# Start-up of a causal convolution with a leaky-ReLU MLP: the second part of x through SyncE in float32 and a GpSimd cast, w_in's far columns and second half behind VectorE's first diagonal

## Chip, cores and metric

One core of a Trainium2 chip. The metric is the device time of one execution in microseconds; the time before is the median of three runs, 681.38 us (681.14 to 681.41).

## What is computed

The input x is float32 of shape (8, 4096, 192): 8 sequences, 4096 tokens, 192 channels in 8 heads of 24. `weight` is (8, 7).

```
w   = softmax(weight, over the 7 taps)            # per head, with 1e-9 added to the sum
y   = sum over k of w[head, k] * x[t - 6 + k]     # causal, zeros ahead of the sequence
h   = y.reshape(32768, 192) @ w_in                # w_in  192 x 2048
g   = max(0.01 * h, h)
out = g @ w_out                                   # w_out 2048 x 192, out float32
```

## The kernel before, in words

**Tiling.** Two sequences (e = 0, 1) are worked on at a time. The 192 channels stand as three chunks c of 64; chunk c of both sequences fills the 128 partitions of the tile xt[rp][:, c, :], with time along the free dimension. A block is 512 tokens of both sequences. To have work for TensorE early, the first two blocks are cut into four groups of 256 tokens, x's first four parts (q = 0 to 3); then whole blocks of 512 follow, 34 groups in all.

**Per group.** VectorE convolves seven taps (`conv_jobs`, L222 for the first tap and L228 for the others, which multiply by columns of wk, the normalized taps), TensorE makes h in PSUM from w_in and y (`mm1`, L507), ScalarE takes it out with Prelu (L515), and TensorE multiplies by w_out (L525 for the first blocks, L588 later), interleaved with the next `mm1`. The convolution of group i+1 is recorded during group i.

**How the parts of x come in.** Part 0 comes over SyncE in float32 (L142), is cast by ScalarE and VectorE (L155), transposed by TensorE and convolved by TensorE too, with diagonal matrices `diag` made from the taps by VectorE (`diag_wide`, L420; the matmuls are L259). Parts 1 and 2 are loaded by GpSimd with a cast during the DMA into `x_rows` (L145), transposed by TensorE (`transpose_first`, L167) and taken out of PSUM by VectorE (`evac_first`, L195). Part 3 and all blocks after it are loaded by GpSimd (L149, L96) and transposed by DMAs of SyncE (L199, L114).

**Weights.** w_in is kept in two halves n of 1024 columns. Rows 0 to 127 go into slot 0 over all partitions and rows 128 to 191 into slot 2 of the lower 64 (`load_w_in`, L316). VectorE, and once ScalarE, copy 64-partition pieces to the other half of the partitions (`spread_up`, L326; `spread_down`, L322), so that each row tile of TensorE finds every chunk. The first half's columns are again split in `near` (the first 512) and `far`.

**What sets the order.** Each engine works through its instructions in the order in which the kernel records them; there is no scheduler (`manual_schedule`), and waits come from data dependences, from `sync`, which adds one by hand, and from the reuse of eight semaphores for GpSimd's DMAs in turn, so that a DMA waits for the landing of the one eight before it. GpSimd's order in the start-up is: select for `sel`; w_in 0 rows 0 to 127 (all 1024 columns); `ident` by a memset and an affine select in `make_identity`; w_in 0 rows 128 to 191 near; x part 1 (two DMAs); w_in 0 rows 128 to 191 far; w_in 1 (two DMAs); x part 2 (two); w_out (two); wk (a sum and a product, L445 and L446); x part 3 (six); block 2 (six).

VectorE's order, after the small work on the taps, is: six diagonals (L420); L326 and L322 for the near columns of w_in 0; y of part 0, chunk 0 (L465); L326, L276, L326; the evacuation of part 1's transposes (L195, twice); L326 for rows 128 to 191 far; the first three taps of part 1's chunk 1 (L222, L228, L228); L322 and L326 twice for the second half of w_in; the remaining taps with one more L326 among them; then y of part 1 from TensorE's convolution of chunks 0 and 2 (L271, L276).

TensorE's order is: warm-up matmuls, the taps' broadcast, the transposes and the convolution of part 0, then `mm1` for group 0 with the transposes of part 1 inside its first pair of column blocks. Its fifth pair is the first that uses the second half of w_in.

Of the kernel before, what the change touches and what calls it, by code (L numbers as in the profile page):

```python
# [10 lines left out]
FP32 = mybir.dt.float32  # L11
BF16 = mybir.dt.bfloat16
# [3 lines left out]
def kernel(  # L16
# [8 lines left out]
    nc = tc.nc  # L25

    B, S, D = x.shape
# [13 lines left out]
    HS = SUB // 2  # L41
    NFC = F // 128
# [3 lines left out]
    RUN = 4  # L46
# [10 lines left out]
    const_pool = ctx.enter_context(tc.tile_pool(name="const", bufs=1))  # L57
    stage_pool = ctx.enter_context(tc.tile_pool(name="stage", bufs=2))
# [17 lines left out]
    x_nat, x_bf, xt = {}, {}, {}  # L76

    def sync(after, first, why):
        tc.add_manual_dep(
            after.ins, first.ins.name,  # L80
            mybir.DependencyInfo(
                mybir.DependencyClass.Sync, mybir.DependencyReason.DATA
            ),
            reason=why,
        )
# [36 lines left out]
    def new_xt(rp):  # L122
# [10 lines left out]
    x_rows = {  # L133
        q: const_pool.tile([128, 2, HS, D], BF16, name=f"x_rows{q}") for q in (1, 2)
    }

    def load_first(q):
        rows = x[0:2, q * HT : (q + 1) * HT, :].rearrange("e (s p) d -> p e s d", s=HS)
        if q == 0:
            x_nat[q] = stage_pool.tile([128, 2, HS, D], FP32, name="x_nat")  # L140
            for s in range(HS):
                nc.sync.dma_start(out=x_nat[q][:, :, s], in_=rows[:, :, s])  # L142
        elif q in x_rows:
            for e in range(2):
                nc.gpsimd.dma_start(out=x_rows[q][:, e], in_=rows[:, e])  # L145
        else:
            for c in range(NCH):
                for e in range(2):
                    nc.gpsimd.dma_start(  # L149
                        out=x_half[q][:, c, :, e, :],  # L150
                        in_=rows[:, e, :, c * CH : (c + 1) * CH],
                    )

    def cast_first(q, s, copy, e=slice(0, 2)):
        copy(  # L155
            out=x_half[q][:, :, s, e, :],
            in_=x_nat[q][:, e, s, :].rearrange("p e (c k) -> p c e k", c=NCH),
        )
# [76 lines left out]
    def y_of(grp, c):  # L235
        blk, t0, T = grp
        if blk not in yt:
            yt[blk] = yt_pool.tile([128, NCH, ST], BF16, name="yt")
        return yt[blk][:, c, t0 : t0 + T]
# [47 lines left out]
    w9 = const_pool.tile([H, K + 1], FP32, name="w9")  # L287
    nc.scalar.dma_start(out=w9[:, 0:K], in_=weight)  # L288
    load_first(0)

    ones = nc.const_aps.tensor(1.0, [128, ST], BF16)
# [7 lines left out]
    for sign, off in ((1, 0), (-1, GRP - 1)):  # L299
        nc.gpsimd.affine_select(  # L300
            out=sel[:, :, 0, :], in_=sel[:, :, 0, :], compare_op=mybir.AluOpType.is_ge,
            fill=0.0, base=off, channel_multiplier=-sign * GRP,
            pattern=[[sign * CH, NCH], [sign, CH]],
# [8 lines left out]
    near, far = slice(0, WF // 2), slice(WF // 2, WF)  # L312

    def load_w_in(n, rows, cols=slice(0, WF)):
        ps, slot = ((0, 128), 0) if rows == 0 else ((0, CH), 2)
        nc.gpsimd.dma_start(  # L316
            out=w_in[n][ps[0] : ps[1], slot, cols],
            in_=moe_w_in[rows : rows + ps[1], n * WF + cols.start : n * WF + cols.stop],
        )
# [8 lines left out]
    def w_in_of(f, e, c, m0, m1):  # L328
# [5 lines left out]
        ]  # L334

    load_w_in(0, 0)
    ident = const_pool.tile([128, 128], BF16)
    make_identity(nc, ident)
    load_w_in(0, 128, near)
    load_first(1)  # L340
    load_w_in(0, 128, far)
    for rows in (0, 128):
        load_w_in(1, rows)
    load_first(2)


    w_out = const_pool.tile([128, NFC, D], BF16)
    for h in range(2):
        cs = slice(h * NFC // (2 * RUN), (h + 1) * NFC // (2 * RUN))
        nc.gpsimd.dma_start(  # L350
            out=w_out.rearrange("p (c i) d -> p c i d", i=RUN)[:, cs],
            in_=moe_w_out.rearrange("(c p i) d -> p c i d", p=128, i=RUN)[:, cs],
        )


    wa = psum_h.tile([128, 2, ST], FP32, name="warm", tag="ph")
# [1 line left out]
    def warm(n, cols=HT, to=wa[:, 0]):  # L358
# [10 lines left out]
        out=nmax, in_=w9[:, 0:K], axis=mybir.AxisListType.X,  # L369
# [3 lines left out]
        out=w9[:, 0:K], in_=w9[:, 0:K], func=mybir.ActivationFunctionType.Exp,  # L373
# [18 lines left out]
    def select(out, parts):  # L392
# [10 lines left out]
    wps_hm = wps_hm[:, :, 0]  # L403
    new_xt(0)
    cast_first(0, 0, nc.scalar.copy)
    cast_first(0, 1, nc.scalar.copy, slice(0, 1))
    cast_first(0, 1, nc.vector.tensor_copy, slice(1, 2))
    taps = const_pool.tile([128, NCH, 2, K + 1, 2], BF16, name="taps")
    nc.vector.tensor_copy(
        out=taps, in_=wps_hm[..., None].to_broadcast([128, NCH, 2, K + 1, 2])  # L410
# [5 lines left out]
    def diag_wide(c, p):  # L416


        shape = [128, K, CH // 2, 2]
        nc.vector.tensor_mul(  # L420
            diag[c][:, p].rearrange("p k (m t) -> p k m t", t=2),
            ident2.rearrange("p (m t) -> p m t", t=2)[:, None].to_broadcast(shape),
            taps[:, c, p, 0:K, None, :].to_broadcast(shape),
        )
# [6 lines left out]
    evac_first(0, nc.scalar.copy, nc.scalar.copy)  # L431
    wml = const_pool.tile([128, NCH, K + 1], FP32, name="wml")
    rsum = const_pool.tile([128, NCH, 1], FP32)
    diag_wide(0, 0)
    diag_wide(0, 1)
    nc.vector.tensor_add(wml, wps_l, taps[:, :, 1, :, 0])
    diag_wide(1, 0)
    nc.vector.scalar_tensor_tensor(
        out=rsum, in0=wml[:, :, K:], scalar=1e-9, in1=taps[:, :, 0, K:, 0],
# [14 lines left out]
    def act_scale(out, in_, scale):  # L454
# [11 lines left out]
        out=y_of(groups[0], 0), in0=hi[:, :HT], scalar=rsum[:, 0, :], in1=low,  # L466
# [301 lines left out]
```

## Time and profile before

| what | value |
|---|---|
| runs: median (lowest to highest) | 681.38 us (681.14 to 681.41) |
| span of the profiled execution, first to last instruction | 679.2 us |
| median of the runs less that span | 2.2 us |
| granted TensorE clock, mean | 1.000 |
| first `mm1` matmul starts | 8.09 us |
| x part 1: issues start; landings | 3.62 and 4.34 us; 7.48 and 8.00 us |
| w_in 0 rows 0 to 127: issue starts; lands | 1.87 us; 6.33 us |
| w_in 1, its two DMAs: land | 12.19 and 12.77 us |
| HBM read, written | 28.31 MB, 25.17 MB |

The profile shows one execution. Times are counted from the span's start; a DMA's landing is the last update of its semaphore. PEld is the loading of weights into TensorE, which overlaps its matmuls (PE). A row of the order of time gives start and duration in microseconds, engine, line, operation, tiles written and read, and how many such instructions were merged; in brackets stand the idle time ahead of it and what ended it. For a DMA on GpSimd the duration is that of its issue (descriptors written), not of the transfer.

### The profile page before, as it was taken

How to read it: one execution, taken by the hardware profiler on the slowest of the kernel's cores; microseconds unless marked ns; L12 is line 12 of the kernel's file. 1: busy time of each engine (PE TensorE's matmuls, PEld its weight loads, DVE VectorE, ACT ScalarE, POOL GpSimd, SP SyncE). 2: the span in 40 equal slices, each digit the busy share in tenths (PEclk: the TensorE clock that was granted, in tenths of full speed). 3: DMA queues.
4: the chain of work that ended last, by engine and by line, in shares of the span. 5: the costliest groups of instructions: out<-in, count | busy, mean ns of one | idle time of the engine just before them, and what ended most of it. 6: DMA issues, size and time to landing. Idle time of an engine off the chain costs nothing.

```text
span 679.2 us, 27092 instructions
## 1 busy us (share of the span) xinstructions
PE 674.9 (99%) x12442; PEld 446.3 (66%) x12442; DVE 481.2 (71%) x816; ACT 517.6 (76%) x601; POOL 147.4 (22%) x208
## 2 busy tenths in 40 slices
PE   9999999999999999999999999999999999999998
PEld 6997666666666666666666666666666666666667
DVE  7989477866768766778667687667786676876612
ACT  7899877777787777777777777778777777777781
POOL 8455221122211222211222112222022220000000
PEclk9999999999999999999999999999999999999999
DMA  9999755655737656556556566567365573321123
GB/s 149 99 119 104 52 85 83 84 64 67 96 74 93 76 54 86 84 85 86 66 63 92 80 92 78 56 83 94 73 87 69 60 96 71 72 56 33 34 49 94
DMA packets 213970, 53.27 MB, mean 78 GB/s; under 512 B 209312, under 2 KB 213536, under 8 KB 213856
## 3 DMA queue, kind: packets, MB, share of 16 engines
q0 software_dynamic: 98832, 13.97, 30.3%
q1 hardware_dynamic: 115008, 37.57, 28.0%
q8 instruction: 97, 1.59, 0.9%
q14 instruction: 17, 0.14, 0.1%
q10 hardware_dynamic: 16, 0.00, 0.0%
HBM read 28.31 MB, written 25.17 MB: 79 GB/s over the span
## 4 chain that ended last, share of the span: by engine, by line
PE 98%; DVE 1%; ACT 0%; issue 0%; ACTq 0%
PE ph L507 49%; PE acc L588 44%; PE po L525 5%; PE acc L259 0%; DVE diag L420 0%; PE ptr L167 0%; ACT L366 0%; ACTq L288 0%; DVE w_in L322 0%; DVE yt L465 0%; DVE o_sb L638 0%; DVE x_half L155 0%; ACT w L372 0%; DVE w_in L326 0%; ACT junk L366 0%
## 5 line engine op out<-in xcount | busy, mean ns | idle before, releaser
L515 ACT ACTIVATE g<-ph 128x1024 bf16<-128x1024 f32 x512 | 496.6, 1021 | 139.8 <-PE ph L507 139.6
L228 DVE SCALAR_TENSOR_TENSOR yt<-xt,wk,yt 128x512 bf16<-128x512 bf16 (+1 forms) x582 | 380.1, 715 | 0.2
L507 PE MATMUL ph<-yt,w_in 64*64 64x512 bf16 (+2 forms) x6048 | 377.5, 369 | 0.3 <-DVE yt L465 0.3
L588 PE MATMUL acc<-g,w_out 64*64 64x512 bf16 x5568 | 339.9, 376 | 0.0
L507 PEld LDWEIGHTS <-w_in 64*64 64x64 bf16 (+1 forms) x6048 | 229.7, 131 | 103.4 <-issue 1.1
L588 PEld LDWEIGHTS <-w_out 64*64 64x64 bf16 x5568 | 178.2, 118 | 118.8
L96 POOL DMA_DIRECT2D x_bf<-in_x_dram x180 | 133.9, 774 | 407.6 <-DMA xt<-x_bf 405.6
L610 DVE STREAM_TRANSPOSE o_t<-acc 128x512 f32<-128x512 f32 x87 | 72.9, 875 | 182.2 <-PE acc L588 182.2
L525 PE MATMUL po<-w_out,g 64*128 64x192 bf16 (+1 forms) x640 | 36.8, 243 | 0.0
L525 PEld LDWEIGHTS <-g 64*128 64x128 bf16 (+1 forms) x640 | 32.6, 95 | 3.2 <-issue 0.4
L222 DVE TENSOR_SCALAR yt<-xt,wk 128x512 bf16<-128x512 bf16 (+1 forms) x97 | 28.8, 320 | 2.4 <-DMA xt<-x_bf 2.4
L598 ACT COPY junk<-junk 128x1 f32<-128x1 f32 x58 | 11.1, 191 | 4.1
L638 DVE COPY o_sb<-po 128x192 f32<-128x192 f32 x8 | 2.8, 356 | 6.8 <-PE po L525 3.9
L638 ACT COPY o_sb<-po 128x192 f32<-128x192 f32 x16 | 5.1, 323 | 0.3
L259 PE MATMUL acc<-xt,diag 64*64 64x256 bf16 x126 | 4.7, 272 | 0.1
L149 POOL DMA_DIRECT2D x_half<-in_x_dram x6 | 4.3, 732 | 0.9 <-DMA w_in<-in_moe_w_in_dram 0.9
L259 PEld LDWEIGHTS <-diag 64*64 64x64 bf16 x140 | 3.7, 106 | 1.0 <-issue 0.4
L360 PE MATMUL warm<-const-bfloat16-1.0 128*128 128x512 bf16 (+2 forms) x8 | 3.3, 577 | 0.8 <-PEq L752 0.8
L145 POOL DMA_DIRECT2D x_rows<-in_x_dram x4 | 2.9, 746 | 0.0
L316 POOL DMA_DIRECT2D w_in<-in_moe_w_in_dram x5 | 2.9, 593 | 0.0
L360 PEld LDWEIGHTS <-const-bfloat16-1.0 128*128 128x128 bf16 x10 | 1.2, 128 | 2.2 <-issue 2.2
L326 DVE COPY w_in<-w_in 64x512 bf16<-64x512 bf16 (+1 forms) x7 | 2.3, 337 | 0.2
(52 smaller groups left out, 25.9 us busy)
## 6 DMA issues: line engine op xcount, KB each, us to landing
out_dram<-o_t SPq DMA_DIRECT2D x112, 192.0 KB, 4.7
x_bf<-in_x_dram POOLq DMA_DIRECT2D x180, 64.0 KB, 3.1
out_dram<-o_sb SPq DMA_DIRECT2D x8, 192.0 KB, 2.8
xt<-x_bf SPq DMA_TRANSPOSE x90, 3.2
w_out<-in_moe_w_out_dram POOLq DMA_DIRECT2D x2, 384.0 KB, 8.3
out_dram<-o_t SPq DMA_DIRECT2D x8, 96.0 KB, 2.4
out_dram<-o_sb SPq DMA_DIRECT2D x8, 96.0 KB, 1.7
w_in<-in_moe_w_in_dram POOLq DMA_DIRECT2D x2, 256.0 KB, 5.5
```

The lines of the kernel that those rows point to most:

```text
L96: ins = nc.gpsimd.dma_start(out=t[:, c, :, e, :], in_=src[2 * rp + e, :, :, c * CH : (c + 1) * CH],)
L222: lambda s=src, d=dst, c=c: nc.vector.tensor_scalar_mul(d, s, wk[:, c, 0:1])
L228: lambda s=src, d=dst, c=c, k=k: nc.vector.scalar_tensor_tensor(out=d, in0=s, scalar=wk[:, c, k : k + 1], in1=d, op0=mybir.AluOpType.mult, ...
L259: lambda k=k, p=p, a=a, ps=ps, to=to, acc=accs[e]: nc.tensor.matmul(out=acc[to, :T], lhsT=diag[c][ps, p, k, :], rhs=xt[0][ps, c, a : a + T ...
L360: nc.tensor.matmul(out=to[:, 0:cols], lhsT=ones[:, 0:128], rhs=ones[:, 0:cols], start=True, stop=True,)
L507: nc.tensor.matmul(out=ph[m : m + M, e, i * T : (i + 1) * T], lhsT=w_in_of(f, e, c, m, m + M), rhs=y[ps, c, t0 : t0 + T], start=(c == chun ...
L515: act = nc.scalar.activation(out=g[blk][:, nf * u : nf * (u + 1), :, t0 : t0 + T], in_=ph.rearrange("p e (i t) -> p i e t", i=nf), func=my ...
L525: return nc.tensor.matmul(out=po[m], lhsT=g[b][ps, fc, e, s * 128 : (s + 1) * 128], rhs=w_out[ps, fc, :], start=start, stop=stop,)
L588: ins = nc.tensor.matmul(out=acc2[gi, r][e * CH : (e + 1) * CH, 0:T], lhsT=w_out_of(ps, fc, r), rhs=g[b][ps, fc, e, t0 : t0 + T], start=fi ...
L598: seal = nc.scalar.copy(out=junk, in_=junk)
L610: nc.vector.transpose(out=osb[gi, 0][:, 0 : T // GB, :, r], in_=acc2.pop((gi, r))[:, 0:T].rearrange("p (j k) -> p j k", k=GB),)
L638: ins = copy(out=o_sb[:, n % 2, :], in_=po.pop(n))
```

## The change

- `load_first(1)` no longer goes through GpSimd with a cast during the DMA. SyncE issues two float32 DMAs, one per sequence, into a second `x_nat` buffer; the first waits for GpSimd's affine select that makes `ident`. `make_identity` is written out for that (a memset and the same select).
- GpSimd asks for w_in 0 rows 128 to 191 near as before. The far columns wait, by `sync`, for VectorE's first `diag_wide`; the second half of w_in follows.
- Then GpSimd casts the two float32 tiles into `x_rows[1]` with two copies of 128x384, and only then come x part 2, w_out, and what stood behind them.
- TensorE's transposes of part 1 wait for the two copies instead of the two DMAs. The order on TensorE, VectorE and ScalarE is the same.

```diff
+        elif q in (1,):
+            x_nat[q] = stage_pool.tile([128, 2, HS, D], FP32, name="x_nat")
+            for e in range(2):
+                ins = nc.sync.dma_start(out=x_nat[q][:, e], in_=rows[:, e])
+                if e == 0:
+                    sync(ins, after, "behind a nearer part")
...
     load_w_in(0, 0)
     ident = const_pool.tile([128, 128], BF16)
-    make_identity(nc, ident)
+    after = nc.gpsimd.memset(ident, 0.0)
+    after = nc.gpsimd.affine_select(
+        out=ident, in_=ident, compare_op=mybir.AluOpType.not_equal, fill=1.0,
+        base=0, pattern=[[-1, 128]], channel_multiplier=1,
+    )
+    load_first(1, after)
     load_w_in(0, 128, near)
-    load_first(1)
-    load_w_in(0, 128, far)
-    for rows in (0, 128):
-        load_w_in(1, rows)
-    load_first(2)
-    w_out = ...
...
-    diag_wide(0, 0)
+    gate = diag_wide(0, 0)
+    sync(load_w_in(0, 128, far), gate, "behind x's second part")
+    for rows in (0, 128):
+        load_w_in(1, rows)
+    for e in range(2):
+        nc.gpsimd.tensor_copy(out=x_rows[1][:, e], in_=x_nat[1][:, e])
+    load_first(2)
+    w_out = ...
     diag_wide(0, 1)
```

More of the change, by code (lines that the diff above doesn't have):

```diff
@@ L135, with load_first @@
     }
-    def load_first(q):
+    def load_first(q, after=None):
         rows = x[0:2, q * HT : (q + 1) * HT, :].rearrange("e (s p) d -> p e s d", s=HS)
@@ L154, in cast_first @@
     def cast_first(q, s, copy, e=slice(0, 2)):
-        copy(
+        return copy(
             out=x_half[q][:, :, s, e, :],
@@ L315, in load_w_in @@
         ps, slot = ((0, 128), 0) if rows == 0 else ((0, CH), 2)
-        nc.gpsimd.dma_start(
+        return nc.gpsimd.dma_start(
             out=w_in[n][ps[0] : ps[1], slot, cols],
@@ L337 @@
     ident = const_pool.tile([128, 128], BF16)
-    make_identity(nc, ident)
-    load_w_in(0, 128, near)
-    load_first(1)
-    load_w_in(0, 128, far)
-    for rows in (0, 128):
-        load_w_in(1, rows)
-    load_first(2)
[L347 to L353, printed above, removed]
+    after = nc.gpsimd.memset(ident, 0.0)
[4 more added lines that the diff above has]
+    load_first(1, after)
+    load_w_in(0, 128, near)
     wa = psum_h.tile([128, 2, ST], FP32, name="warm", tag="ph")
@@ L419, in diag_wide @@
         shape = [128, K, CH // 2, 2]
-        nc.vector.tensor_mul(
+        return nc.vector.tensor_mul(
             diag[c][:, p].rearrange("p k (m t) -> p k m t", t=2),
@@ L433 @@
     rsum = const_pool.tile([128, NCH, 1], FP32)
-    diag_wide(0, 0)
+    gate = diag_wide(0, 0)
[5 more added lines that the diff above has]
+    load_first(2)
+    w_out = const_pool.tile([128, NFC, D], BF16)
+    for h in range(2):
+        cs = slice(h * NFC // (2 * RUN), (h + 1) * NFC // (2 * RUN))
+        nc.gpsimd.dma_start(
+            out=w_out.rearrange("p (c i) d -> p c i d", i=RUN)[:, cs],
+            in_=moe_w_out.rearrange("(c p i) d -> p c i d", p=128, i=RUN)[:, cs],
+        )
     diag_wide(0, 1)
```

## The prediction

> **What bounds the kernel now.** I read the page first, then the windows by stage, then the order of time of GpSimd and VectorE in the first 16 us, and last who waits there.
>
> Page, part 1 (busy time, share of the span) and part 4 (the chain that ended last, by engine):
>
> ```profile
> PE 674.9 (99%) x12442; PEld 446.3 (66%) x12442; DVE 481.2 (71%) x816; ACT 517.6 (76%) x601; POOL 147.4 (22%) x208
> ...
> PE 98%; DVE 1%; ACT 0%; issue 0%; ACTq 0%
> ```
>
> TensorE is the bound: 674.9 of 679.2 us, at a granted clock of 1.00 throughout. From the first matmul on w_in (8.09 us) to the last stage it is never idle for long, so a microsecond can be won or lost only where it waits, before 8.09 and in the few waits shortly after. A stall there moves everything behind it, since nothing later is idle enough to give it back. The change touches only work of the first 16 us.
>
> Windows by stage (width, busy us of PE, PEld, DVE, ACT, POOL; clock; DMA share; GB/s):
>
> ```profile
> 0.00:8.09 8.09, 6.83 (x106) 4.36 (x107) 5.12 (x25) 4.92 (x12) 7.27 (x19) 1.00 0.79 133
> 8.09:16.50 8.41, 8.41 (x166) 6.43 (x167) 7.36 (x19) 7.40 (x10) 6.74 (x12) 1.00 1.19 165
> ```
>
> In both windows GpSimd is nearly full (7.27 of 8.09, 6.74 of 8.41): it is a queue of instructions in order, and whatever the change inserts pushes back all that stands behind. GpSimd in order of time (start, duration, what):
>
> ```profile
> 3.62 1.44 POOL L145 DMA_DIRECT2D x_rows<-in_x_dram  x2
> 5.03 1.67 POOL L316 DMA_DIRECT2D w_in<-in_moe_w_in_dram  x3
> 6.64 1.48 POOL L145 DMA_DIRECT2D x_rows<-in_x_dram  x2
> 8.05 1.48 POOL L350 DMA_DIRECT2D w_out<-in_moe_w_out_dram  x2
> 9.46 0.32 POOL L445 TENSOR_TENSOR wk<-taps,wml 128x21 f32<-128x21 bf16 x1
> 9.87 0.22 POOL L446 TENSOR_TENSOR wk<-wk,rsum 128x21 f32<-128x21 f32 x1
> 10.09 1.48 POOL L149 DMA_DIRECT2D x_half<-in_x_dram  x2
> 12.47 2.87 POOL L149 DMA_DIRECT2D x_half<-in_x_dram  x4 [0.91 <-DMA w_in<-in_moe_w_in_dram]
> ```
>
> The line to keep in mind is wk, done at 10.09. VectorE's convolution of the second part of x reads it:
>
> ```profile
> 9.88 0.36 DVE L326 COPY w_in<-w_in 64x512 bf16<-64x512 bf16 x1
> 10.26 0.29 DVE L222 TENSOR_SCALAR yt<-xt,wk 128x256 bf16<-128x256 bf16 x1
> 10.59 1.00 DVE L228 SCALAR_TENSOR_TENSOR yt<-xt,wk,yt 128x256 bf16<-128x256 bf16 x2
> 12.21 0.42 DVE L322 COPY w_in<-w_in 64x1024 bf16<-64x1024 bf16 x1 [0.61 <-DMA w_in<-in_moe_w_in_dram]
> 12.64 0.77 DVE L326 COPY w_in<-w_in 64x512 bf16<-64x512 bf16 x2
> ```
>
> wk has 0.17 us to spare before 10.26. Behind its three reads VectorE sits idle 0.61 us until w_in's second half lands, then spreads it over the partitions, and TensorE waits for exactly that:
>
> ```profile
> 13.46 1.02 PEld L507 LDWEIGHTS <-w_in 64*128 64x128 bf16 x19 [0.21 <-DVE w_in L326]
> ```
>
> Of these 0.21 us 0.11 is the ordinary step (12 such matmuls take 0.65 us, two at a time), so TensorE loses 0.1: it could have gone on at 13.36.
>
> **The change, part by part.**
>
> *x's second part by SyncE.* Removed from GpSimd: the two issues at 3.62 (to 5.03, 1.41 us). SyncE has nothing between 1.77 and 18.1 us, so nothing queues behind its wait for the select at 2.85+0.29 = 3.14; it issues at about 3.2 and 3.65 (0.45 each, as for x's first part). What arrives sooner is not what was late: by the landing records the two x_rows loads land at 7.48 and 8.00 (3.62 + 3.9, 4.34 + 3.7), TensorE's transposes start at 8.65. Gain on the path: nothing.
> Landing in float32: x's first part landed 2.6 us after each issue with the DMA engines almost empty, which gives 5.8 and 6.25; the most is the present 8.0, since the same bytes and w_in's first half are read from HBM either way. I take 7.2 for the second, between the two, because w_in's 512 KB are in flight until 6.33. The Trainium skill (DMA: Bandwidth & Descriptors, "Issuing engines are not separate DMA queues") speaks against a gain: DMAs of all issuers share the same engines and another issuer saves only the time to issue; by it x would land near 8.0, at the late end.
> w_in's first part lands at 6.33 and VectorE takes it at 6.67: 0.3 us of room for what x now takes from it. Beyond that each 0.1 us is 0.1 us at 8.09.
>
> *The gate.* The far columns wait for the first diagonal (4.52 + 0.39 = 4.91, start about 4.95, against 5.03 now): 0.08 us earlier, because the 1.41 us removed and the wait for 4.91 fill the same time. Behind the waiting instruction stand all later GpSimd work: w_in, casts, x's third part, w_out, wk. The three w_in issues take 6.64 - 5.03 = 1.61 and end at 6.56.
>
> *The casts, new on GpSimd.* The trace has no copy on GpSimd. Nearest rows: memsets of 128x128 and 128x192 at 228 and 258 ns give 0.35 us for 384 columns (lower bound); selects at 287 and 355 ns, which read and write, give 355 + 192 x 1.06 = 0.56; two selects of 192 give 0.71 (upper). I take 0.56, as a copy reads and writes too, with 0.07 between instructions: 1.25 for both, 0.8 to 1.5. They start at 6.6 if x has landed, or the second at 7.2 to 8.0 by the landing. They end at 7.8, or 7.8 to 8.6 by the landing; with some mutual blocking with VectorE's copies I take 8.0. TensorE's transposes need them at 8.65: 0.6 in hand.
>
> *What is queued behind the casts.* From the first issue of x's third part to wk's first instruction 9.46 - 6.64 = 2.82, wk itself 10.09 - 9.46 = 0.62. So wk is done at 8.0 + 2.82 + 0.62 = 11.44, L222 starts at 11.47 in place of 10.26: **1.21 us late.** From L222 to TensorE's resumption is 13.46 - 10.26 = 3.20, of which 0.61 is the wait for w_in; w_in is now there long before, so 2.59 remain: TensorE resumes at 14.06 in place of 13.46, **0.6 us late**. The wait for a DMA has turned into a wait for wk. The two do not add: 0.61 of the 1.21 is swallowed.
>
> *Mutual blocking.* Copy L322 of 64x512 at 6.97 took 550 ns, L326 of the same shape at 6.67 only 287; GpSimd was issuing x's third part (6.64 to 8.12). L326 of 64x1024 at 12.85 took 559, L322 of that shape 422. So GpSimd can hold up such a copy by 0.14 to 0.26 us. The casts now meet L326 and L322 at 6.67 and 6.97. At best the copies go unhindered (0.26 less), at worst each waits for a whole cast: 2 x 0.56 - 0.26 = 0.86 more. The first matmul then moves from 8.09 by -0.1 to +0.86 (no earlier than that, as the second chunk's scale on ScalarE ends only at 8.18). I take +0.2. It is covered: with TensorE waiting to 14.06, up to 0.7 us of lateness at 8.09 vanish in the same stall. Without that cover it would count in full. The Trainium skill (SBUF — State Buffer, "Who interferes with whom") says that a VectorE copy in a two-port mode and a GpSimd operation lock each other out for the whole instruction; the rows above show 0.26 at most, and by the rule the estimate would be the upper end.
>
> *x's third part, w_out, x_half.* Their issues come 1.3 us later. The third part is used at 15.98 and landed at 13.28 and 13.81. x_half's issues now wait 0.91 us for w_in and the next block's loads 0.68 and 1.08 us for w_out's landing; those waits swallow the delay, and w_out still lands behind the same bytes. I cost them at nothing; if w_out slipped, the first use is at 17.1, 1.4 after its first landing at 15.73.
>
> **Sum.** Removed issues and earlier landing 0; gate -0.08 (already in 8.0); wk +0.6; blocking covered. The page gives the span, 679.2; the runs' median is 681.38, 2.2 us more for what lies around it, which I take as fixed. 679.2 + 0.6 + 2.2 = **682.0 us**, +0.09%.
>
> **Rivals.**
>
> 1. *Hidden.* Casts at 0.35 us with x there by 6.6 end at 7.4; wk at 10.84, TensorE resumes at 13.46. For it: x landing 2.6 us after issue. Against: 0.56 from the select. Time 681.3.
> 2. *The start decides.* The casts block L326 and L322 in full, or w_in's first part lands past 6.67; the first matmul moves to 8.8 or 8.95 and less than that is left of the wk stall. For it: 550 against 287 ns. Time 681.38 + 0.8 = 682.2.
> 3. *Slower by over 0.2%: x starves.* x and w_in share the DMA engines, the second x lands past 8.2 and a cast takes 0.7 with blocking, so the casts end past 8.8. Then wk is past 12.2, TensorE resumes past 14.86, 1.4 late; from there each 0.1 us of landing costs 0.1. For it: DMA digits of 9 in the first two slices of the page. Against: the same bytes land by 8.00 today. Time 683.0.
> 4. *The change does nothing for x:* transposes were not waiting for it (8.00 against 8.65); this is part of the forecast, whose sign comes only from what the casts push back.
>
> **How the numbers follow.** wk late by a stall of 0.2 to 1.2 us: 0.62. Rival 1: 0.14. Rival 2: 0.09. Rival 3: 0.13. Something faster by over 0.2% (1.36 us, about what a measurement of this kernel can tell from no change): 0.02, since only 0.1 + 0.1 us of waits are there to win. Slower by over that: rival 3 with little else, 0.14. Within: 0.84. Range: from the unhindered end (681.38 - 0.2) to rival 3 (683.0): 681.1 to 683.0.
>
> **What would show it.** Right: two copies on GpSimd of about 0.5 us from 6.6 to 8.0; wk at about 11.4; L222 of VectorE waiting for POOL wk some 1 us; L322 of the second half with no wait for the DMA; TensorE's wait for DVE w_in of 0.8 in place of 0.21. Wrong: wk before 10.9, a first matmul after 8.9, transposes that wait for POOL, or a difference after 16.5 us.

## The result, and the profile after

The changed kernel takes 682.52 us (median of 14 runs, 682.14 to 682.89); the kernel before, run beside it, 681.01 (14 runs, 680.63 to 681.44). The ratio is 1.0021, with a 95% interval of 1.0014 to 1.0029: **1.5 us slower**. The profiled execution spans 680.9 us, 1.77 more than before. The lines of the changed kernel's program are about six to ten higher: `mm1` is L517, the first tap L228, the other taps L234, spread_up and spread_down L332 and L328, wk L455 and L456, y of part 0 L465 and L475.

The page of the kernel after, parts 1 and 4:

```profile
PE 675.5 (99%) x12442; PEld 447.4 (66%) x12442; DVE 481.7 (71%) x816; ACT 517.7 (76%) x601; POOL 146.8 (22%) x208
...
PE 93%; DVE 5%; POOL 1%; DMA 1%; issue 0%; SPq 0%; POOLq 0%
```

Busy times are those of before, 675.5 against 674.9, so the time went into waits. Part 4 says whose: the chain that ended last was 98% TensorE and 1% VectorE; now it has VectorE 5%, GpSimd 1% and a DMA 1%. Which, the windows by stage tell first (columns as in the prediction):

```profile
0.00:8.09 8.09, 7.05 (x110) 4.47 (x111) 5.10 (x25) 4.93 (x12) 4.94 (x16) 1.00 0.73 156
8.09:16.50 8.41, 7.42 (x143) 5.45 (x141) 5.95 (x16) 6.28 (x9) 8.33 (x14) 1.00 1.10 159
```

GpSimd has gone from 7.27 to 4.94 us in the first window and from 6.74 to 8.33, which is full, in the second; there TensorE has gone from 8.41 to 7.42. The chain of waits of the kernel after shows the path through that hole (start, length, what):

```profile
3.58 4.44 DMA x_nat<-in_x_dram
...
8.07 0.28 POOL x_rows L436
8.35 0.17 issue
8.52 1.43 POOL x_rows L151 x2
9.95 1.42 POOL w_out L441 x2
11.37 0.27 POOL wk L455
11.63 0.07 issue
11.70 0.23 POOL wk L456
...
11.96 0.30 DVE yt L228
```

x's second DMA lands at 8.02, the cast follows, then four DMA issues that nothing on this path needs, then wk, and only then VectorE's first tap. The two casts of this kernel in order of time, each started by a landing:

```profile
7.30 0.50 POOL L436 CAST x_rows<-x_nat 128x384 bf16<-128x384 f32 x1 [0.52 <-DMA x_nat<-in_x_dram]
8.07 0.51 POOL L436 CAST x_rows<-x_nat 128x384 bf16<-128x384 f32 x1 [0.26 <-DMA x_nat<-in_x_dram]
```

The other end of the chain, VectorE and then TensorE's weight loads in order of time:

```profile
9.84 0.29 DVE L332 COPY w_in<-w_in 64x512 bf16<-64x512 bf16 x1
11.96 0.29 DVE L228 TENSOR_SCALAR yt<-xt,wk 128x256 bf16<-128x256 bf16 x1 [1.82 <-POOL wk L456]
12.28 1.01 DVE L234 SCALAR_TENSOR_TENSOR yt<-xt,wk,yt 128x256 bf16<-128x256 bf16 x2
13.32 0.42 DVE L328 COPY w_in<-w_in 64x1024 bf16<-64x1024 bf16 x1
13.76 0.78 DVE L332 COPY w_in<-w_in 64x512 bf16<-64x512 bf16 x2
```

```profile
12.97 0.11 PEld L517 LDWEIGHTS <-w_in 64*128 64x128 bf16 x1 [0.20 <-issue]
14.26 0.15 PEld L517 LDWEIGHTS <-w_in 64*128 64x128 bf16 x4 [1.18 <-DVE w_in L332]
14.59 0.47 PEld L517 LDWEIGHTS <-w_in 64*128 64x128 bf16 x10 [0.18 <-DVE w_in L332]
```

L328 at 13.32 has no bracket: w_in's second half landed long before (10.21 and 10.86, where it was 12.19 and 12.77). The wait of 0.61 us for a DMA became one of 1.82 us for wk. TensorE stands 1.18 us ahead of 14.26, and what it did from 13.46 on it now does from 14.59 on.

Matching TensorE's matmuls one by one with those of before gives the whole sum, for these two executions:

| point in TensorE's program | after less before, us | what made it |
|---|---|---|
| first `mm1` | -0.28 (7.82 for 8.09) | L328 took 0.29 instead of 0.55 |
| from 9.1 to 13 us | -0.03 | the second chunk waits for ScalarE's L465 as before |
| resumption at 14.6 | +1.13 | the wait above |
| behind 47 us | +1.41 | VectorE's taps are late there too, in this execution |
| end of the span | +1.77 | SyncE's last waits |

The step at 47 us is in the chain of waits:

```profile
44.95 2.66 DVE yt L234 x4
47.61 0.04 issue
47.65 1.27 PE ph L517 x10
```

In before VectorE convolved without a gap from 17.9 to 46.16 and was done 0.1 us ahead of TensorE. Here it is 1.44 late and TensorE only 1.13, so TensorE waits 0.28. Of VectorE's lateness 1.13 came with the start. Another 0.10 came at 19 us, where one first tap took 456 ns for 286 and the next 322 for 515, and 0.23 at 34.58, where one took 577 ns for 335. GpSimd was issuing a load of the next block beside them (18.70 to 19.45, 34.25 to 35.04); that this is the cause was not tried, and a first tap of before took 335 ns beside such an issue (33.37 to 33.70). The step is not a steady effect of the change: in the traces of two other changed kernels that lost as much at 13 us (1.14 and 1.02, below "two output DMAs fewer" and "SyncE asks for x at once") it is 0.02 and 0.01, in a third ("the casts read x part 0") 0.27, and in one of a variant of the kernel before ("wk first in the kernel before") 0.18.

The last step lies behind TensorE's last matmul: from its start to the end of the span 3.57 us instead of 3.21. SyncE then goes through the semaphores of its DMAs in a fixed turn. From the two traces, the start of each of those waits (* is released by the last landing, the others had nothing to wait for or were released earlier):

```
before  677.00 .06 .12 .18 .25 .31 .37 .43  678.25*                       drain 678.32
after   678.41 .57 679.66*  .72 .79 .85 .91 .97 680.03                    drain 680.09
```

Each wait costs 0.06 us, even if its semaphore is long set. In before the last landing is at the last place; two more DMAs on SyncE (x part 1) move it on by two, to a place with six waits behind it, 679.66 to 680.03 or 0.37 us. The twelve profiled executions of this case agree: in the five kernels with two SyncE DMAs more than before the stretch behind the last matmul is 3.56 to 3.57 us, in the other seven 3.19 to 3.21.

### The profile page after: what moved, and what is told of

Its sections match the earlier page's. It is cut to its first block, busy times and chain, and to the rows that moved or that the text cites. A ratio compares the mean times of both kernels' runs of the same rounds, so it can differ in the third digit from the quotient of the medians.

```text
span 680.9 us, 27094 instructions
## 1 busy us (share of the span) xinstructions
PE 675.5 (99%) x12442; PEld 447.4 (66%) x12442; DVE 481.7 (71%) x816; ACT 517.7 (76%) x601; POOL 146.8 (22%) x208
## 4 chain that ended last, share of the span: by engine, by line
PE 93%; DVE 5%; POOL 1%; DMA 1%; issue 0%; SPq 0%; POOLq 0%
PE ph L517 46%; PE acc L598 44%; DVE yt L234 4%; PE po L535 3%; DMA x_nat<-in_x_dram 1%; DVE yt L228 0%; POOL x_rows L151 0%; POOL w_out L441 0%; DVE w_in L332 0%; DVE yt L282 0%; POOL sel L306 0%; POOL w_in L322 0%; DVE xt L201 0%; DVE w_in L328 0%; DVE yt L277 0%
## 5 line engine op out<-in xcount | busy, mean ns | idle before, releaser
L234 DVE SCALAR_TENSOR_TENSOR yt<-xt,wk,yt 128x512 bf16<-128x512 bf16 (+1 forms) x582 | 381.6, 730 | 0.2
L517 PE MATMUL ph<-yt,w_in 64*64 64x512 bf16 (+2 forms) x6048 | 378.3, 369 | 1.2 <-DVE w_in L332 1.0
L517 PEld LDWEIGHTS <-w_in 64*64 64x64 bf16 (+1 forms) x6048 | 230.3, 131 | 104.4 <-issue 1.5
L228 DVE TENSOR_SCALAR yt<-xt,wk 128x512 bf16<-128x512 bf16 (+1 forms) x97 | 29.7, 335 | 3.9 <-POOL wk L456 1.8
L322 POOL DMA_DIRECT2D w_in<-in_moe_w_in_dram x5 | 2.8, 567 | 1.6 <-DVE diag L417 1.6
L332 DVE COPY w_in<-w_in 64x512 bf16<-64x512 bf16 (+1 forms) x7 | 2.2, 328 | 0.2
```

The costliest lines, as they stand in the source:

```text
L228: lambda s=src, d=dst, c=c: nc.vector.tensor_scalar_mul(d, s, wk[:, c, 0:1])
L234: lambda s=src, d=dst, c=c, k=k: nc.vector.scalar_tensor_tensor(out=d, in0=s, scalar=wk[:, c, k : k + 1], in1=d, op0=mybir.AluOpType.mult, ...
L517: nc.tensor.matmul(out=ph[m : m + M, e, i * T : (i + 1) * T], lhsT=w_in_of(f, e, c, m, m + M), rhs=y[ps, c, t0 : t0 + T], start=(c == chun ...
```

## The experiments

Theory 1: GpSimd's queue. wk is late because casts, landing and issues stand ahead of it. Rival A: contention, x in float32 and w_in sharing the DMA engines, or the casts holding up VectorE. Rival B, found in the trace after: the end of the kernel, nothing to do with the start. All were run beside the kernel before; medians are of 11 or 12 runs.

**wk ahead of the casts.** The casts, x part 2 and w_out (not shown) go behind wk, the work is the same:

```diff
-    for e in range(2):
-        nc.gpsimd.tensor_copy(out=x_rows[1][:, e], in_=x_nat[1][:, e])
-    load_first(2)
...
     nc.gpsimd.tensor_add(wk, taps[:, :, 0, 0:K, 0], wml[:, :, 0:K])
     nc.gpsimd.tensor_mul(wk, wk, rsum.to_broadcast([128, NCH, K]))
+    for e in range(2):
+        nc.gpsimd.tensor_copy(out=x_rows[1][:, e], in_=x_nat[1][:, e])
+    load_first(2)
...
     load_first(3)
```

> The changed kernel with wk's sum and product ahead of the casts on GpSimd; casts, x's third part and w_out behind them. Theory 1 (queue): TensorE's stall of 1.2 us at 13 us is wk, pushed back by what the change puts ahead of it. Then wk runs at 6.8 to 7.4 us, while GpSimd waits for x anyway, VectorE's first tap (L222 of before) starts at about 10.2 instead of 11.96, TensorE's wait for VectorE's spread of w_in's second half goes from 1.2 us to 0.1 or nothing, VectorE has no late convolution at 47 us, and the time falls by 1.1 to 1.4 us to 681.1 to 681.4. The 0.36 us at the end of the profiled span stay. Theory 2 (contention): the float32 loads and the casts hold up w_in and VectorE's copies; moving wk takes less than 0.3 us off 682.5.

681.5 us against 681.0, ratio 1.0008 (0.9999 to 1.0016): 1.0 of the 1.5 us is gone. GpSimd and VectorE of this kernel in order of time:

```profile
6.80 0.27 POOL L445 TENSOR_TENSOR wk<-taps,wml 128x21 f32<-128x21 bf16 x1
7.14 0.22 POOL L446 TENSOR_TENSOR wk<-wk,rsum 128x21 f32<-128x21 f32 x1
7.84 1.10 POOL L448 CAST x_rows<-x_nat 128x384 bf16<-128x384 f32 x2 [0.48 <-DMA x_nat<-in_x_dram]
```

```profile
10.37 0.29 DVE L332 COPY w_in<-w_in 64x512 bf16<-64x512 bf16 x1
10.69 0.45 DVE L228 TENSOR_SCALAR yt<-xt,wk 128x256 bf16<-128x256 bf16 x1
```

wk fits into the time in which GpSimd waits for x, with 0.48 us of that wait left, and the first tap starts behind VectorE's own copy, with no wait. x landed no sooner (7.79 and 8.29). Of the 0.5 us that remain 0.36 is the end of the span, so what the late x costs by itself is too small to be seen here.

**Two output DMAs fewer.**

```diff
-            parts = 2 if gi == len(groups) // 2 else 1
+            parts = 2 if gi == len(groups) // 2 and e else 1
```

> The changed kernel with two output DMAs of SyncE fewer in the middle group, so that the number of SyncE's DMAs is that of before and the last one falls on the semaphore that it had there. If the 0.36 us at the end come from the order in which SyncE goes through its eight DMA semaphores (six more waits of 0.06 us behind the last landing), the time falls by 0.36 us to about 682.15 and the stretch behind the last landing is as long as before; TensorE's matmuls keep their 1.1 to 1.4 us. If the end is long because of anything else (a later landing, the outputs' DMAs), it stays at 682.5.

682.23 against 681.0, ratio 1.0019 (1.001 to 1.0027); 0.29 less than the changed kernel, and the trace has 3.20 us behind the last matmul instead of 3.57. The difference of the medians is less than half the spread of either kernel (0.75 and 0.69 us), so the trace carries this one.

**The same tail put on the kernel before,** by two more output DMAs:

```diff
-            parts = 2 if gi == len(groups) // 2 else 1
+            parts = (4 if e else 1) if gi == len(groups) // 2 else 1
```

> The kernel before with two more output DMAs of SyncE in the middle group (the same bytes cut finer), so that the last DMA falls two semaphores further on, as in the changed kernel. If the order of the last waits is what costs, +0.36 us (681.4), all of it behind the last landing, and TensorE's matmuls unmoved. Otherwise 681.0.

681.39 against 681.09, ratio 1.0003 (0.9995 to 1.0012); 3.56 us behind the last matmul. The median moved by 0.30, the tail in the trace by 0.35; the interval of the ratio alone would not exclude that nothing moved.

**Both repairs on the changed kernel.**

> Both edits. Theory 1: the two add, 682.5 - 1.1 to 1.4 - 0.36 = 680.75 to 681.05, at or a little under the time of before (681.0), since w_in's second half lands at 10.2 and 10.9 in place of 12.2 and 12.8 and TensorE's wait of 0.1 us for its spread can go. Theory 2: 682.1.

680.98 against 681.0, ratio 1.0004 (0.9993 to 1.0016; one of 12 runs, at 685.47, stands apart). TensorE's matmuls lie 0.26 us behind those of before at 12 us and 0.05 behind them from 16 us to the end, the span is 679.2, and part 4 is back to TensorE alone:

```profile
PE 99%; ACT 0%; DVE 0%; issue 0%
```

With wk's place and the last semaphore mended, the rest of the change costs and gains nothing that these runs can tell.

**wk first in the kernel before,** its sum and product moved ahead of x part 2 and w_out in the same way.

> The kernel before with wk's sum and product ahead of x's third part and w_out on GpSimd. Theory 1: wk at 7.3 us instead of 10.09 has no reader before 10.26, when VectorE comes free, and w_in's second half lands at 12.2 as before; no change within 0.15 us (681.0). It shows whether wk bound anything in the kernel before. If wk's place counts only where it is late, this is nothing while the same edit is worth over a microsecond in the changed kernel.

681.16 against 681.09, ratio 1.0001 (0.9992 to 1.0009). wk ended at 7.42 instead of 10.09 and nothing came of it: in before wk was not what VectorE waited for.

**The gate alone,** in the kernel before (x part 1 still by GpSimd):

```diff
-    load_w_in(0, 128, far)
-    for rows in (0, 128):
-        load_w_in(1, rows)
-    load_first(2)
...
-    diag_wide(0, 0)
+    gate = diag_wide(0, 0)
+    sync(load_w_in(0, 128, far), gate, "behind the first diagonal")
+    for rows in (0, 128):
+        load_w_in(1, rows)
+    load_first(2)
```

> The kernel before with the gate alone: w_in's far columns and second half behind VectorE's first diagonal, x's second part by GpSimd with the cast in the DMA as before. The gate as such costs GpSimd 0.15 to 0.25 us (it starts the far columns at about 5.2 instead of 5.03); wk is done at 10.3, VectorE's first tap at 10.3 instead of 10.26, and its wait for w_in at 12.2 swallows it: 681.0, no change within 0.15. If the gate itself were what cost the microsecond, 682.

681.1 against 681.09, ratio 1.0 (0.9991 to 1.0009). The diagonal ended at 4.975, the far issue began at 5.268, and wk ended at 10.38.

**SyncE asks for x at once,** without waiting for GpSimd's select:

```diff
-                if e == 0:
-                    sync(ins, after, "behind a nearer part")
```

> The changed kernel without the wait of SyncE for the select: x's second part is asked for at 1.8 and 2.2 us, right behind the first. Theory 1: it lands some 1 us or more before 7.25 and 8.02, the casts run from 6.8 to 7.9, wk is done at 11.25 in place of 11.92, and TensorE's stall is 0.6 us shorter: about 681.9. What it takes from w_in's first part shows as a later landing than 6.37; beyond 6.65 VectorE's first copy and the first matmul move, which the stall at 13 us covers. Theory 2: w_in's first part lands so late (past 7.5) that the first matmul moves past 8.6 and the gain is gone: 682.5 or more.

682.19 against 681.0, ratio 1.0017 (1.0009 to 1.0026). x was asked for at 1.82 and 2.33 instead of 3.17 and 3.58 and landed at 7.09 and 7.92 instead of 7.25 and 8.02:

```profile
7.14 0.50 POOL L434 CAST x_rows<-x_nat 128x384 bf16<-128x384 f32 x1 [0.30 <-DMA x_nat<-in_x_dram]
7.97 0.51 POOL L434 CAST x_rows<-x_nat 128x384 bf16<-128x384 f32 x1 [0.32 <-DMA x_nat<-in_x_dram]
```

The request came 1.3 us earlier and the landing 0.10 to 0.16 us, which is less than one execution differs from the next: in the five changed kernels that ask at 3.2 and 3.6 us the second landing lies between 7.71 and 8.29. w_in's first part came 0.5 later (6.87; 5.83 to 6.45 in those five). So rival A has one part that is true: here the landing was not set by the time of asking. The last kernel of this section shows the other side, a landing that moves with the bytes asked for ahead of it.

**The casts read x part 0,** which has landed (so the output's part 1 is made of part 0's values):

```diff
-        nc.gpsimd.tensor_copy(out=x_rows[1][:, e], in_=x_nat[1][:, e])
+        nc.gpsimd.tensor_copy(out=x_rows[1][:, e], in_=x_nat[0][:, e])
```

> The changed kernel, in which the two casts read x's first part, which landed long before, in the place of the second (the second part's values are so replaced by the first part's, and nothing waits for the second part's landing). If the wk that comes late is made of the landing that the casts wait for, the casts go one behind the other from the end of the third issue of a weight, 6.8, to 7.85, wk ends near 11.2 instead of 11.92, the first tap starts near 11.25, and TensorE resumes at 13.9 instead of 14.6: about 681.8 to 681.9 us. If what counts is the time that the casts and the issues themselves take, with the landing hidden, wk stays at 11.9 and the time at 682.5. The last 3.57 us behind TensorE's last matmul stay in both.

681.8 against 681.2, ratio 1.0009 (1.0001 to 1.0018): 0.7 below the changed kernel. wk ended at 11.16. But it no longer set the end: the first `mm1` started at 8.52, 0.43 late, and that lateness went through. GpSimd, then VectorE, of this kernel:

```profile
6.76 1.04 POOL L436 CAST x_rows<-x_nat 128x384 bf16<-128x384 f32 x2
```

```profile
5.95 0.97 DVE L417 TENSOR_TENSOR diag<-ident,taps 128x448 bf16<-128x448 bf16 x2
6.95 0.48 DVE L332 COPY w_in<-w_in 64x512 bf16<-64x512 bf16 x1
7.45 0.50 DVE L328 COPY w_in<-w_in 64x512 bf16<-64x512 bf16 x1
7.98 0.48 DVE L475 SCALAR_TENSOR_TENSOR yt<-acc,rsum,low 128x256 bf16<-128x256 f32 x1
```

Casts that come in time meet VectorE's copies, and each copy takes 0.48 to 0.50 us instead of 0.29. Both ends lie 0.15 us behind the end of a cast (7.283 and 7.437; 7.798 and 7.948). So the landing at 8.02 makes wk about 0.75 us late (11.92 for 11.16), and at the same time it keeps the casts clear of the copies; the 0.7 us between the two medians hold both.

**Two casts in the kernel before,** into a tile that nothing reads:

```diff
+    for e in range(2):
+        nc.gpsimd.tensor_copy(out=x_spare[:, e], in_=x_nat[0][:, e])
     load_first(2)
```

> The kernel before, with two casts on GpSimd of 128x384 float32 each, of x's first part into a tile that nothing reads, ahead of the issues of x's third part; nothing else is changed. The casts alone cost GpSimd's queue 2 x 0.51 and two gaps of 0.03: wk ends near 11.2 instead of 10.09, the first tap starts near 11.25 instead of 10.26. By the theory of the queue TensorE then resumes between 13.8 and 14.0 instead of 13.46 (a part of the 1.1 us lies under the wait for w_in's second half, which ends at 12.77 to 12.9), and the time is 681.4 to 681.6; the end behind TensorE's last matmul stays 3.2 us. If the casts cost by locking a port that VectorE needs, VectorE's copies between 6.8 and 7.9 get longer and the first matmul starts later than 8.1, with the same size of loss at the start and none at 13 us.

681.56 against 681.2, ratio 1.0005 (0.9996 to 1.0014); the median is in the forecast band, but the run does not separate the theories. wk ended at 11.20, as the queue has it. The first `mm1` started at 8.85, 0.75 late: 0.45 of that was there before the casts began (two diagonals took 0.70 and 0.59 us instead of 0.39 and 0.38 while GpSimd issued DMAs), and 0.30 came with them (a diagonal of 0.75 us and a copy of 0.48). TensorE then had no wait at 13 us. Queue and blocking lead to the same 0.6 us here, so which of them decides can't be read from it.

**A trial for a better version:** the kernel before with wk first, and w_in's far columns of the first 128 rows asked for behind x part 1.

```diff
-    load_w_in(0, 0)
+    load_w_in(0, 0, near)
...
     load_first(1)
+    load_w_in(0, 0, far)
```

> The kernel before with wk's sum and product ahead of the issues of x's third part and of w_out, and with the far columns of the first rows of w_in asked for behind x's second part. wk ends near 7.9, the first tap no longer waits for it, and the near columns land sooner, so that the first matmul may start 0.2 us sooner. If the start is paid by the order of the requests alone, 680.6 to 680.9 us; if the far columns land too late for ScalarE's copy, which starts at 8.7, or if the wait for w_in's second half at 12.8 takes it up, no difference from 681.0.

681.48 against 681.2, ratio 1.0006 (0.9997 to 1.0015). The profiled execution, the shortest of its eleven, is 0.24 us shorter than before (678.9), the medians are not. It shows what moves x's landing: part 1, asked for at the same 3.62 and 4.34 us, landed at 6.54 and 7.22 instead of 7.48 and 8.00, with half of w_in's first 512 KB now asked for behind it. In the five profiled executions with all 512 KB ahead of a load of part 1 by GpSimd, the second landing lies between 8.00 and 8.37. No version faster than the kernel before was found.

## Why the prediction was right, and where its sum was short

**Right: the mechanism.** TensorE bounds, the gain of x by SyncE is nothing (the transposes started at 8.55 for 8.65), and the casts push GpSimd's queue until the wait for w_in has turned into one for wk. The kernel with wk first takes that away, and 1.0 us with it. The two casts took 504 and 508 ns where 560 was taken. w_in's second half no longer made VectorE wait, as forecast. Rival 1 (hidden) would have needed x by 6.6; it came at 7.25. Rival 2 (the start decides) did not occur in the changed kernel, but its mechanism did, in the two kernels whose casts ran early. Rival 3 (x starves) had the right direction: the second landing was 8.02, short of its 8.2, and the casts ended at 8.58 and not past 8.8.

**The failing term: x's landing.** The step said "I take 7.2 for the second". It was 8.02, and 7.71 to 8.29 in the five profiled executions of kernels with this load, against 8.00 to 8.37 in five with GpSimd's own DMA. From there the miss of the stall follows: casts end 8.58 for 8.0, the queue from there to wk's end is 0.1 shorter than the 3.44 taken (3.35), wk is done at 11.92 for 11.44, and TensorE resumes 1.13 late instead of 0.6. The transposes' 0.6 us in hand were gone too: they started at 8.55, as the second cast ended. Nothing swallows the extra half microsecond, since the 0.61 us of cover was already spent. The 7.2 lay between a row with empty DMA engines (2.6 us) and the present 8.0. For a transfer that shares the engines with 512 KB of w_in the second row was the nearer one: 1.3 us of earlier asking moved the landing by 0.1, and 256 KB fewer ahead of it moved it by 0.8. The rule that was weighed and set aside, the Trainium skill's "Issuing engines are not separate DMA queues" (DMA: Bandwidth & Descriptors), held here: the new issuer brought the second landing forward by 0.2 us on the mean of five executions each (8.00 for 8.20), which is within their scatter.

**The gate** was to start the far issue 0.04 us behind the diagonal. It took 0.29 (4.892 to 5.185), and 0.29 again in the kernel with the gate alone. Rows of before had shown it: x_half began at 12.47, where the landing that it waited for was at 12.19. It did not matter for wk, as GpSimd then stood idle 0.52 us for x.

**Blocking** was taken at +0.2 and was -0.28, because the late x kept the casts (from 7.30) behind the copies (to 7.25), and GpSimd, which in before was issuing DMAs beside L322, stood idle from 6.78. That the price itself is real, the two kernels with early casts show: +0.2 per copy. The prediction held 0.26 for the most that a row showed and set the longer lock of the Trainium skill (SBUF — State Buffer, "Who interferes with whom") at the upper end. The five copies of these traces that began 0.22 to 0.45 us ahead of the end of a running cast all ended 0.14 to 0.15 us behind that end, as an exclusive lock held to the end of the instruction would have it. That it is a port for which they wait is shown by no run here.

**Missed: "a difference after 16.5 us".** The prediction named it as what would prove it wrong, and by that sign it had a term too few: +0.36 us at the end of the span, which it put at nothing by holding that the change touches only the first 16 us. It was shown both ways, by taking two DMAs away and by adding two. The profiled execution has a second such difference, +0.28 at 47 us, where VectorE had only 0.1 us in hand; since two other changed kernels with about the same stall don't have it, it is not shown to belong to the change. The sum: 0.60 forecast + 0.53 (landing and what follows from it) + 0.28 + 0.36 = 1.77, the difference of the two spans. The medians differ by 1.51.

**What lies around the span** was taken as fixed at 2.2 us. The changed kernel's profiled execution has 682.64 - 680.93 = 1.7, and so has every run on record less its own span (1.65 to 1.79); the 2.2 came from setting a median of three runs against the span of a faster execution. The later medians of before, 681.0 to 681.2, are 0.2 to 0.4 under the 681.38 that the forecast started from. That error went against the others, which is luck: 682.0 missed 682.52 by 0.5, while the forecast of the difference, 0.6, missed 1.5 by 0.9.

## What to carry to other kernels

Before you put a wait or slow work into an engine's queue, list what stands behind it and who reads that: here 0.5 us of wk, which fitted into an idle gap ahead of the casts, cost 1.0 us behind them. Take the landing of a transfer from a row of the same stage with the same traffic, not from one with empty engines; here another issuer hardly moved it, and fewer bytes ahead of it did. Count DMAs on the queue whose semaphores the kernel's end goes through: two more at the start were 0.36 us at the end.

## What the runs showed of the hardware

- A GpSimd DMA began 0.28 to 0.29 us after what it waited for (4.892 to 5.185, 4.975 to 5.268; a landing in before, 17.585 to 17.869); GpSimd's own cast 0.05 after a landing (8.015 to 8.068), a VectorE instruction 0.03 after wk (11.924 to 11.958).
- A VectorE bf16 copy that began 0.22 to 0.45 us ahead of the end of a running GpSimd cast ended 0.14 to 0.15 us behind that end (five cases; 7.798 to 7.948), but VectorE's y of part 0 (float32 from PSUM, L475, 7.28 to 7.76) took its usual 0.48 us beside a cast (7.30 to 7.81).
- TensorE's matmuls of part 0's convolution ran at half pace for the first 0.4 to 1.1 us in 3 of the 12 profiled executions, with the granted clock at 1.00; why these three is not known. The same window of before and of the kernel with two output DMAs fewer, 40 matmuls against 20:

```profile
5.60:6.40 0.80, 0.80 (x40) 0.73 (x36) 0.80 (x5) 0.14 (x1) 0.80 (x2) 1.00 1.20 133
```

```profile
5.60:6.40 0.80, 0.80 (x20) 0.67 (x24) 0.80 (x6) 0.00 (x0) 0.80 (x3) 1.00 0.92 193
```

  In these three the first `mm1` came at 8.31, 8.56 and 8.70. With the change's stall at 13 us nothing of this is left (0.47 us late at the start, 1.14 behind the stall, where the changed kernel has 1.13). In the kernel with the gate alone, which has no such stall, it went through (0.61 late at the start, 0.69 from 16 us on). That this is why the runs of before spread more (680.63 to 681.97 over all, against 682.14 to 682.89) was not tested.
